# Loading k plainly and turning it on TensorE, one load queue in order of need, list-ordered layernorm: a change to the opening of a fused attention and gated-MLP kernel

## The chip, the cores and the metric

The kernel runs on one NeuronCore of one Trainium2 chip. The metric is the device time of one execution in microseconds (us). A change counts as faster or slower when the time moves by over 2%.

## The reference

```python
def reference(A_x, A_wqkv, A_w_phi, A_wo, B_x, B_w_gate, B_w_up, B_w_down):
    x  = A_x                                  # (1, 2048, 512) bf16
    xn = layernorm(x)                         # no scale, eps 1e-5
    # A: linear attention, H = 32 heads of 16, features = [softmax(k@w_phi), softmax(-k@w_phi)]
    #    kv = sum over s of phi_k^T v,  z = sum of phi_k,  o = (phi_q kv) / (phi_q z + 1e-6),  A = o @ wo
    # B: (xn@w_gate * xn@w_up) @ w_down       # F = 1792
    return x + A(xn, wqkv, w_phi, wo) + B(xn, w_gate, w_up, w_down)
```

## The kernel before

The kernel records steps with their reads and writes; a list scheduler then orders each engine. TensorE's order is fixed by the order of the recording, and so are steps recorded with `pin` set. The tokens come in 16 tiles of 128. To "turn" is to transpose; a "DMA turn" is a transpose made by a DMA, a copy that runs beside the engines; PSUM banks are the memory into which TensorE writes. `xn` is the normalised tile, `xnT` its turned form, `Wp` the product of the k (or q) weights with the block-diagonal `w_phi`, made once by `w_fold`; it needs the k weights turned. A "unit" (`up_unit`) is one gate/up pair of 4 + 4 matmuls of 128x512 into two PSUM banks, then a ScalarE copy and a VectorE multiply.

```python
    sc.pin = True                               # loads; SP and ACT are the two load queues
    load_x(0, 1)
    load_w(ACT, wv_v, ...)                      # 512 KB
    load_x(1, 1)
    load_x(2, 2)
    load_w(ACT, wphi_v, ...)
    load_qkT(1)                                 # k weights by a transposing DMA, SP queue
    load_gu(ACT, 0)                             # gate/up columns 0..255
    load_x(4, 4)
    load_gu(SP, 1)
    load_gu(SP, 2)                              # 1 MB
    load_x(8, 4)
    # ... (cut)
    sc.pin = True                               # the opening
    warm(16)
    ln_stats(0, 1); ln_stats(1, 1); ln_apply(0); ln_apply(1); ln_stats(2, 1); ln_stats(3, 1)
    x_transpose(0); x_transpose(1)
    ln_apply(2); ln_apply(3)
    v_matmul(0, 0)                              # v of tile 0 into PSUM bank 0
    v_matmul(1, 1)                              # v of tile 1 into PSUM bank 1
    x_transpose(2); x_transpose(3)
    for dt in range(NQ):
        w_fold(1, dt, (2, 3, 6, 7)[dt])
    sc.pin = False
    up()                                        # first unit, then the loop over tiles

    for t in range(NT + 2):                     # the loop, shortened
        if t < NT: features("ek", t, 1)         # matmul, two Exps, VectorE reduce ...
        if t % 2 == 0 and 4 + t < NT: ln_stats(4 + t, 2)
        up(); x_next(t + 4); late_loads(t)      # t == 5: w_down and wo, 2.3 MB
        # ... v_matmul(t - 1), v_scale(t - 1)
        if t < 2: v_scale(t, t)                 # reads PSUM bank t
        else:
            up(); kv_acc(t - 2); up()           # kv_acc writes PSUM banks 0 and 1
    # ... (cut)
    q_next(6)
    up(len(ups))                                # the units that are left
    num_stage(0)
    q_next(7)
    for t in range(1, NT):
        num_stage(t); out_tile(t - 1); q_next(t + 7)
    out_tile(NT - 1, 2)
```

Note for later: `kv_acc` of tile 0 may not start before `v_scale` of tile 1 has emptied bank 1.

The softmax here doesn't subtract the row's maximum and nothing guards it: scores larger than these inputs give would overflow.

## Time and profile before

| | |
|---|---|
| time, median of 4 runs | 230.68 us (230.38 to 231.04) |
| span in the profile | 228.0 us; that execution took 229.74 us, faster than all timed ones |
| TensorE busy | 96% |
| first gate/up unit on TensorE | 16.37 us |
| first kv accumulation | 27.6 us |

The page's head and slices. Each digit is the busy share of one fortieth of the span in tenths; PEclk is the granted TensorE clock in tenths.

```profile
span 228.0 us, 3302 instructions
PE 218.7 (96%) x1266; PEld 105.7 (46%) x1266; DVE 146.9 (64%) x276; ACT 83.3 (37%) x161; POOL 45.3 (20%) x77
PE   7389999999999999999999999989999999999995
DVE  2768998658546674667678456587776767635341
PEclk9979999999999999999999999999999999999999
```

TensorE is at 8 tenths or more from the third slice to the last but one, so only the opening, one small hole near slice 27 and the tail of 2.5 us can give anything.

The timeline of the opening, some lines (start in us, duration in us, engine, line, operation, output and input, count, and in brackets the idle time before it and what ended it; DVE is VectorE, ACT ScalarE, PE TensorE):

```profile
5.64 0.69 DVE L335 BATCH_NORM_STATS2 arena<-arena 128x6 f32<-128x512 bf16 x1 [1.57 <-DMA arena<-in_A_x_dram]
9.86 1.06 ACT L193 ACTIVATE arena<-ps 128x512 bf16<-128x512 bf16 x2
10.49 3.29 PE L212 MATMUL ps<-arena 128*128 128x512 bf16 x8 [2.26 <-ACT arena L193]
15.47 1.05 PE L314 MATMUL ps<-arena 128*128 128x128 bf16 x16 [0.96 <-ACT arena L193]
16.37 9.88 PE L212 MATMUL ps<-arena 128*128 128x512 bf16 x45
19.17 1.29 DVE L335 BATCH_NORM_STATS2 arena<-arena 128x6 f32<-128x512 bf16 x2 [0.18 <-DMA arena<-in_A_x_dram]
27.59 0.42 PE L423 MATMUL ps<-arena 128*128 128x68 bf16 x8
```

In order: statistics of x tile 1, late because its load shared the engines with wv; the first copies of turned x; the eight v matmuls at about half speed (0.41 us each against 0.216 later); the folds; the units; the statistics of x tile 8, which start almost without a wait; and the first kv accumulation (L423).

All waits of TensorE in that profile (who waits for whom: us in total, times, longest):

```profile
PE ps L212 <- ACT arena L193: 2.3, 1, 2.3
PE ps L536 <- DVE arena L273: 1.3, 1, 1.3
PE ps L365 <- DVE arena L345: 1.2, 2, 0.8
PE ps L212 <- DVE arena L500: 1.0, 1, 1.0
PE ps L314 <- ACT arena L193: 1.0, 1, 1.0
```

The only one after the opening is the 1.0 us for L500, the last gating multiply, at 150.5 us: the features of tile 7 want the bank it reads.

### The profile page before, as it was taken

The page shows a single profiled execution, that of the slowest core. Times are in us where ns is not written, and L with a number is a line of the kernel's source. Part 1 is how long each engine was busy: PE and PEld are TensorE (multiplying, and loading weights), DVE is VectorE, ACT ScalarE, POOL GpSimd, SP SyncE. Part 2 cuts the span into 40 slices and gives each one's busy share as a digit, 9 for nine tenths or more (in the row PEclk, how much of TensorE's full clock was granted, in tenths as well). Part 3 has the DMA queues.
Part 4 walks back from the last instruction along what each step waited for, and adds up shares of the span by engine and source line. Part 5 has one row for each costly group of instructions (what it writes and reads, how often), then busy time and mean ns, then how long its engine had stood idle before and what let it go on. Part 6 is the DMA issues. An engine that isn't in the chain of part 4 may idle for free.

```text
span 228.0 us, 3302 instructions
## 1 busy us (share of the span) xinstructions
PE 218.7 (96%) x1266; PEld 105.7 (46%) x1266; DVE 146.9 (64%) x276; ACT 83.3 (37%) x161; POOL 45.3 (20%) x77
## 2 busy tenths in 40 slices
PE   7389999999999999999999999989999999999995
PEld 3144444444444444444444444444444454454454
DVE  2768998658546674667678456587776767635341
ACT  3459467673343444335524434441111122000000
POOL 3210433403022201212242210131113211100000
PEclk9979999999999999999999999999999999999999
DMA  6997955990000000000220120228654545562221
GB/s 185 304 348 147 294 109 155 329 115 3 0 3 0 0 0 3 0 1 0 49 47 12 34 42 6 46 46 116 139 115 94 95 92 116 112 100 54 67 67 46
DMA packets 48513, 19.91 MB, mean 87 GB/s; under 512 B 37360, under 2 KB 48496, under 8 KB 48496
## 3 DMA queue, kind: packets, MB, share of 16 engines
q1 hardware_dynamic: 46384, 18.62, 36.5%
q10 hardware_dynamic: 2112, 1.07, 1.8%
q8 instruction: 10, 0.16, 0.3%
q14 instruction: 7, 0.06, 0.1%
HBM read 8.67 MB, written 2.10 MB: 47 GB/s over the span
## 4 chain that ended last, share of the span: by engine, by line
PE 92%; DVE 2%; DMA 2%; ACT 2%; issue 1%; SPq 0%; DVEq 0%
PE ps L212 88%; DMA arena<-in_A_x_dram 2%; PE ps L423 2%; PE ps L466 2%; ACT arena L193 2%; PE ps L314 1%; DVE arena L335 1%; DVE arena L500 0%; DVE arena L336 0%; DVE arena L345 0%; DVE arena L387 0%; PE ps L365 0%; DVE arena L517 0%; SPq L234 0%; DVEq L724 0%
## 5 line engine op out<-in xcount | busy, mean ns | idle before, releaser
L212 PE MATMUL ps<-arena 128*128 128x512 bf16 (+1 forms) x946 | 208.0, 377 | 3.3 <-ACT arena L193 2.3
L212 PEld LDWEIGHTS ps<-arena 128*128 128x128 bf16 x946 | 90.3, 98 | 103.5 <-ACT arena L193 2.4
L193 ACT ACTIVATE arena<-ps 128x512 bf16<-128x512 f32 (+1 forms) x128 | 70.0, 597 | 100.0 <-PE ps L212 95.6
L387 DVE TENSOR_REDUCE arena<-arena 128x64 f32<-128x1024 bf16 x32 | 38.7, 1214 | 20.7 <-ACT arena L193 20.7
L500 DVE TENSOR_TENSOR arena<-ps,arena 128x512 bf16<-128x512 f32 x56 | 38.3, 685 | 21.3 <-PE ps L212 20.8
L397 POOL TENSOR_TENSOR arena<-arena 128x512 bf16<-128x512 bf16 x32 | 33.7, 1055 | 67.9 <-DVE arena L395 61.1
L517 DVE TENSOR_TENSOR arena<-ps,arena 128x512 bf16<-128x512 f32 (+1 forms) x17 | 11.2, 660 | 23.7 <-PE ps L212 23.7
L410 POOL CAST arena<-arena 128x32 bf16<-128x32 f32 x16 | 5.1, 321 | 64.8 <-DVE arena L391 48.9
L193 ACT ACTIVATE arena<-arena 128x2 f32<-128x2 f32 (+2 forms) x32 | 13.8, 460 | 9.6 <-DVE arena L336 5.8
L335 DVE BATCH_NORM_STATS2 arena<-arena 128x6 f32<-128x512 bf16 x16 | 10.4, 675 | 4.9 <-DMA arena<-in_A_x_dram 4.9
L478 DVE TENSOR_TENSOR arena<-ps,arena 128x512 bf16<-128x512 f32 x16 | 11.1, 691 | 0.5
L411 DVE TENSOR_TENSOR arena<-ps,arena 128x512 bf16<-128x512 f32 x16 | 10.4, 649 | 0.1
L391 DVE RECIPROCAL arena<-arena 128x64 f32<-128x64 f32 x16 | 8.6, 538 | 0.0
L423 PEld LDWEIGHTS ps<-arena 128*128 128x128 bf16 x128 | 6.2, 97 | 3.8
L466 PEld LDWEIGHTS ps<-arena 128*128 128x128 bf16 x128 | 6.2, 97 | 3.8
L395 DVE TENSOR_TENSOR arena<-arena 128x32 f32<-128x32 f32 x32 | 6.8, 213 | 0.4
L423 PE MATMUL ps<-arena 128*128 128x68 bf16 x128 | 6.7, 194 | 0.0
L466 PE MATMUL ps<-arena 128*128 128x68 bf16 x128 | 6.7, 194 | 0.0
L536 PE MATMUL ps<-arena 128*128 128x512 bf16 x16 | 5.0, 480 | 1.3 <-DVE arena L273 1.3
L477 DVE RECIPROCAL arena<-arena 128x32 f32<-128x32 f32 x16 | 5.6, 353 | 0.5
L350 POOL TENSOR_SCALAR arena<-arena 128x1 f32<-128x1 f32 x12 | 2.9, 265 | 15.1 <-ACT arena L193 15.1
L393 DVE RECIPROCAL arena<-arena 128x32 f32<-128x32 f32 x16 | 5.6, 349 | 0.3
(22 smaller groups left out, 25.9 us busy)
## 6 DMA issues: line engine op xcount, KB each, us to landing
out_dram<-arena SPq DMA_DIRECT2D x15, 128.0 KB, 1.7
arena<-in_B_w_down_dram SPq DMA_DIRECT2D x1, 1792.0 KB, 8.0
arena<-in_A_x_dram SPq DMA_DIRECT2D x3, 512.0 KB, 6.4
arena<-in_B_w_gate_dram SPq DMA_DIRECT2D x3, 512.0 KB, 5.5
arena<-in_B_w_up_dram SPq DMA_DIRECT2D x3, 512.0 KB, 6.4
arena<-arena SPq DMA_TRANSPOSE x44, 3.0
arena<-in_A_wqkv_dram ACTq DMA_DIRECT2D x1, 512.0 KB, 4.2
arena<-in_A_wo_dram SPq DMA_DIRECT2D x1, 512.0 KB, 8.9
```

The lines of the kernel that those rows point to most:

```text
L193: return sc.step(ACT, lambda e: e.activation(out=out_ap, in_=in_ap, func=func, scale=scale, **kw), reads, writes, 130.0 + 0.833 * n)
L212: ins = e.matmul(out_ap, lhsT=l, rhs=r, start=start and i == 0, stop=stop and i == npair - 1, **kw)
L335: dve(lambda e, t=t: e.bn_stats(stats_v[:, t, 0:6], x_tile(t)), [("x", t)], [("st", t)], 512)
L387: dve(lambda e: e.tensor_reduce(out=sm, in_=e_v, axis=AX.X, op=ALU.add), [(name, s, 0), (name, s, 1)], [("sums", sr)], 1024)
L391: dve(lambda e: e.reciprocal(out=rs, in_=sm), [("sums", sr)], [("rs", s)], 64, 6.5)
L397: pool(lambda e: e.tensor_tensor(out=e_v[:, :, 1, :], in0=e_v[:, :, 1, :], in1=rat[:, :, None].to_broadcast([128, H, 16]), op=ALU.mult), [ ...
L411: dve(lambda e: e.tensor_tensor(out=vs_tile(t)[:, :, 0:16], in0=bank(b).rearrange("p (h f) -> p h f", h=H), in1=rp.unsqueeze(2).to_broadca ...
L423: ins = e.matmul(bank(c // 4, (c % 4) * CW, CW), lhsT=ek[:, c * 128:(c + 1) * 128], rhs=vs[:, c * CW:(c + 1) * CW], start=(t == 0 and c % ...
L466: ins = e.matmul(bank(b0 + c // 4, (c % 4) * CW, CW), lhsT=ph[:, c, :], rhs=kvz_v[:, c, :], start=True, stop=True)
L478: dve(lambda e: e.tensor_tensor(out=o_tile(t).rearrange("p (b h f) -> p b h f", b=2, f=16), in0=nd[:, :, :, 0:16], in1=w_v[:, r].unsqueeze ...
L500: dve(lambda e: e.tensor_tensor(out=hT_v[:, ft, sg * 512:(sg + 1) * 512], in0=bank(bu), in1=g, op=ALU.mult), [("ps", bu), ("g", s)], [("hT ...
L517: dve(lambda e, ps=ps, stg=stg, cs=cs: e.tensor_tensor(out=stg, in0=ps, in1=x_tile(t)[:, cs], op=ALU.add), [("ps", bk), ("x", t)], [("ostg ...
```

## The change

Intent: bring the opening to an end earlier. The first x tiles no longer share the DMA engines with wv, the transposing DMA of the k weights (4.94 us of issue time on the SP queue) goes away for 16 cheap turns on TensorE, all loads stand in one queue in order of need, and the layernorm steps of the first tiles are placed by the scheduler. Two units stand in front of the loop instead of one.

```diff
     load_x(0, 1)
-    load_w(ACT, wv_v, A_wqkv[:, 1024:1536]..., "wv", 524288)
-    load_x(1, 1)
+    load_x(1, 1, ACT)
     load_x(2, 2)
     load_w(ACT, wphi_v, ...)
-    load_qkT(1)
-    load_gu(ACT, 0)
+    load_w(SP, wk_v, A_wqkv[:, 512:1024]..., "wk", 524288)
+    load_w(SP, wv_v, A_wqkv[:, 1024:1536]..., "wv", 524288)
+    load_gu(SP, 0)
     load_x(4, 4)
     load_gu(SP, 1)
     load_gu(SP, 2)
 ...
+    def wk_transpose(jt, b):                    # four 128x128 turns, then a ScalarE copy
+        ...
 ...
-    sc.pin = True
-    warm(16)
-    ln_stats(0, 1) ... ln_apply(3)              # fixed order, see above
-    v_matmul(0, 0)
-    v_matmul(1, 1)
-    x_transpose(2)
-    x_transpose(3)
-    for dt in range(NQ):
-        w_fold(1, dt, (2, 3, 6, 7)[dt])
-    sc.pin = False
-    up()
+    for t in range(4):
+        ln_stats(t, 1)
+        ln_apply(t)
+    warm(11)
+    x_transpose(0, 2)
+    x_transpose(1, 3)
+    wk_transpose(0, 4)
+    wk_transpose(1, 6)
+    wk_transpose(2, 7)
+    wk_transpose(3, 2)
+    v_matmul(0, 0)
+    x_transpose(2, 3)
+    x_transpose(3, 4)
+    v_matmul(1, 1)
+    w_fold(1, 0, 2)
+    w_fold(1, 1, 3)
+    up()
+    w_fold(1, 2, 2)
+    w_fold(1, 3, 3)
+    up()
 ...
     q_next(6)
-    up(len(ups))
+    up(len(ups) - 1)
     num_stage(0)
+    up()
     q_next(7)
 ...                                             # _order: 50 instead of 200 ns after a step of the same engine
```

More of the change, by code (lines that the diff above doesn't have):

```diff
@@ L147, in _build @@
     alloc("zero", 512, at=layout["hT"])
+    alloc("wk", NQ * 512, at=layout["hT"] + (NF - 1) * S_TOK)
     alloc("wphi", NQ * 16)
@@ L156, in _build @@
     alloc("rstd", 2 * NT)
+    alloc("nbias", 2 * NT)
     alloc("lnv", 2 * NT)
-    alloc("nbias", 2 * NT)
+    alloc("eps", 2 * 2)
     alloc("sums", 2 * 16 * 64)
@@ L163, in _build @@
     alloc("w", 2 * 4 * 32)
-    alloc("eps", 2 * 2)
     total = (cur[0] + 31) // 32 * 32
@@ L228, in xnT, with load_x @@
         return sb("xnT", q * S_TOK + lo, n)
-    def load_x(t0, n):
+    def load_x(t0, n, eng=SP):
         o = sb("x", t0 * 512, n * 512).rearrange("p (t d) -> p t d", t=n)
         i = x_flat[t0 * 128:(t0 + n) * 128, :].rearrange("(t p) d -> p t d", p=128)
-        sc.dma(SP, lambda e: e.dma_start(o, i), [], [("x", t) for t in range(t0, t0 + n)], n * 131072)
+        sc.dma(eng, lambda e: e.dma_start(o, i), [], [("x", t) for t in range(t0, t0 + n)], n * 131072)
     wT_v = sb("wT", 0, 2 * NQ * 512).rearrange("p (w j d) -> p w j d", w=2, j=NQ)
+    wk_v = sb("wk", 0, NQ * 512).rearrange("p (q j) -> p q j", q=NQ)
     wv_v = sb("wv", 0, NQ * 512).rearrange("p (q j) -> p q j", q=NQ)
@@ L248, in load_qkT @@
         o, i = wT_v[:, w], A_wqkv[:, w * 512:(w + 1) * 512]
-        sc.dma(SP, lambda e: e.dma_start_transpose(o, i), [], [("wT", w)], 524288)
+        sc.dma(SP, lambda e: e.dma_start_transpose(o, i), [], [("wT", w, j) for j in range(NQ)], 524288)
     def load_gu(eng, s):
@@ L258, in _build @@
     load_x(0, 1)
-    load_w(ACT, wv_v, A_wqkv[:, 1024:1536].rearrange("(q p) j -> p q j", p=128), "wv", 524288)
-    load_x(1, 1)
+    load_x(1, 1, ACT)
     load_x(2, 2)
@@ L263, in _build @@
            "wphi", 16384)
-    load_qkT(1)
-    load_gu(ACT, 0)
+    load_w(SP, wk_v, A_wqkv[:, 512:1024].rearrange("(q p) j -> p q j", p=128), "wk", 524288)
+    load_w(SP, wv_v, A_wqkv[:, 1024:1536].rearrange("(q p) j -> p q j", p=128), "wv", 524288)
+    load_gu(SP, 0)
     load_x(4, 4)
@@ L306, in _build, with fn @@
     Wp_v = sb("Wp", 0, 2 * NQ * 512).rearrange("p (w q f) -> p w q f", w=2, q=NQ)
+    def wk_transpose(jt, b):
+        def fn(e):
+            ins = None
+            for dt in range(NQ):
+                ins = e.transpose(bank16(b, dt * 128, 128), wk_v[:, dt, jt * 128:(jt + 1) * 128], ident)
+            return ins
+        sc.step(PE, fn, ["wk", "ident"], [("ps", b)], 4 * 60.0)
+        act(wT_v[:, 1, jt, :], bank16(b, 0, 512), [("ps", b)], [("wT", 1, jt)])
     def w_fold(w, dt, b=None):
@@ L316, in fn @@
             return ins
-        sc.step(PE, fn, [("wT", w)] + [("wbd", jt) for jt in range(NQ)], [("ps", b)], 4 * 60.0)
+        sc.step(PE, fn, [("wT", w, jt) for jt in range(NQ)] + [("wbd", jt) for jt in range(NQ)], [("ps", b)], 4 * 60.0)
         if dt % 2 == 0:
@@ L325, in _build @@
     mv_v = sbf("mv", 0, NT * 2).rearrange("p (t k) -> p t k", t=NT)
-    lnv = sbf("lnv", 0, NT)
     rstd = sbf("rstd", 0, NT)
     nbias = sbf("nbias", 0, NT)
+    lnv = sbf("lnv", 0, NT)
     def xn_tile(t):
@@ L357, in x_turn, with x_transpose @@
         sc.dma(SP, lambda e: e.dma_start_transpose(o, xn_tile(t)), [("xn", t % 4)], [("xnT", t)], 131072)
-    def x_transpose(t):
-        b = misc_bank()
+    def x_transpose(t, b):
         def fn(e):
@@ L448, in q_transpose @@
         src = sb("eq", s * 1024, 1024)
-        wk = [("wT", 0), ("wT", 1)] if t < RP else []
+        wk = [("wT", w, j) for w in range(2) for j in range(NQ)] if t < RP else []
         sc.dma(SP, lambda e: e.dma_start_transpose(ph_tile(t), src), reads, [("phT", t % RP)] + wk, 262144, free=wk)
@@ L500, in up_unit @@
         dve(lambda e: e.tensor_tensor(out=hT_v[:, ft, sg * 512:(sg + 1) * 512], in0=bank(bu), in1=g, op=ALU.mult),
-            [("ps", bu), ("g", s)], [("hT", ft, sg)] + (["zero"] if ft == 0 and sg == 0 else []), 512)
+            [("ps", bu), ("g", s)], [("hT", ft, sg)] + (["zero"] if ft == 0 and sg == 0 else []) + (["wk"] if ft == NF - 1 and sg == 0 else []), 512)
     def out_tile(t, parts=1):
@@ L538, in warm @@
         sc.step(PE, fn, ["zero"], [("ps", 5)], n * 320.0)
-    sc.pin = True
-    warm(16)
-    ln_stats(0, 1)
-    ln_stats(1, 1)
-    ln_apply(0)
-    ln_apply(1)
-    ln_stats(2, 1)
-    ln_stats(3, 1)
-    x_transpose(0)
-    x_transpose(1)
-    ln_apply(2)
-    ln_apply(3)
+    for t in range(4):
[8 more added lines that the diff above has]
+    wk_transpose(3, 2)
     v_matmul(0, 0)
+    x_transpose(2, 3)
+    x_transpose(3, 4)
     v_matmul(1, 1)
-    x_transpose(2)
-    x_transpose(3)
-    for dt in range(NQ):
-        w_fold(1, dt, (2, 3, 6, 7)[dt])
-    sc.pin = False
+    w_fold(1, 0, 2)
[3 more added lines that the diff above has]
+    w_fold(1, 3, 3)
     up()
@@ L678, in _order @@
             remaining[d.idx] -= 1
-            ready_time[d.idx] = max(ready_time[d.idx], st.finish + LAT)
+            ready_time[d.idx] = max(ready_time[d.idx], st.finish + (LAT if d.lane != st.lane else 50.0))
             if remaining[d.idx] == 0:
```

## The prediction

> **What bounds it now.** The page gives PE 96% busy. The timeline shows why: from 16.5 to 225.5 us TensorE runs its list with one visible gap, 1.05 us at 150.5 (the features of tile 7 wait for the last gating multiply). 128x512 matmuls follow each other every 0.216 us. So only the opening 16.5 us, that gap and a tail of 2.5 us can give anything; the change adds no work to the long middle.
>
> **The opening before.** The chain of waits: tile 1 of x lands at 5.6 us, because its 128 KB share the DMA engines with the 512 KB of wv issued earlier on the other queue (the Trainium skill, "DMA: Bandwidth & Descriptors", Issuing engines are not separate DMA queues, says that such DMAs interleave on the same 16 engines; this trace agrees: x0 alone took 2.3 us, x1 4.4). Layernorm then turns xT0 at 7.0; four Ln/Exp pairs stand before the first PSUM copies on ScalarE (9.86); v matmuls start at 10.5 and take 3.29 us for 8 (0.41 each, granted clock 0.72 over 10.5-16.5) after 2.3 us of idle. The skill, "TensorE: Matmul & The Clock Gate", Part 1, says that an idle array drops to half clock; these 0.41 against 0.216 agree. Then turns, copies, four folds; gate/up work starts at 16.53. The transposed k load (issue 4.9 us, landing after 7.9) lands by 10.1, not last.
>
> **What the change does.** It removes the 512 KB DMA transpose and five warm-up matmuls; adds 16 128-column PE transposes (about 1 us) and four ScalarE copies (0.54 us each); moves x1 ahead of the weights, interleaves the layernorm, and starts one unit after two folds.
>
> Estimate from the trace's durations: x1 lands by about 3.6; xT0 turns near 5.9; wk lands near 6.2, wv near 7.7, both before they are needed. ScalarE becomes the chain: eight copies and the last Exps in a row, from 6.7 to about 11.8. First gate/up unit near 11.9, two folds (0.5 us) still to come: continuous work begins the equivalent of **4.1 us earlier**, v matmuls at full clock included.
>
> **What is given back.** VectorE was 91% busy in 16.5-28. Its list after has the statistics of tile 8 before the reduction of tile 0 and the third multiply, but the load of tile 8 is near the end of the same 5.2 MB and can land little earlier (19.1 before; I estimate 18.5). VectorE should idle about 2 us there, and the backlog makes TensorE wait near 26 us for a PSUM bank: about 0.9 us (0.3 to 1.5). At the end of the ups, the gap of 1.05 us shrinks to about 0.25, but the first output tile then arrives about 0.85 us before its transposed o: net zero.
>
> **Prediction: 227.6 us** (4.1 − 0.9 saved from 230.78), 8 in 10 between 226.0 and 229.4. Faster by over 2%: 0.13; within 2%: 0.86; slower: 0.01.
>
> **What would show it.** Right: tile 1 statistics start before 4 us; the first multi-unit matmul at 11.5-12.5; ScalarE solid from 6.7 to 11.8; no clock drop; VectorE waiting 1-2 us for the x load near 17-18.5; PE waiting for the multiply once near 26; PE waiting for the transposed o near 153 minus the gain. Wrong: clock below 0.9 between 7 and 14; PE waiting for wk or wv; no VectorE wait for x.
>
> **What would make it wrong.** TensorE is only about 60% busy between 5 and 12 us; if the clock halves there, 1 to 2.5 us are lost. If tile 8 lands early or TensorE never catches up with VectorE, nothing is given back: 226.7. If wk or wv land 2 us later than estimated, the start slips alike.

## The result, and the profile after

The changed kernel took 227.95 us (median of 4 runs, 227.71 to 228.13) against 230.68 us. The ratio is 0.988, 95% interval 0.9863 to 0.9898. Ratios in this document are the mean time of one kernel's fast runs over that of the other's of the same rounds, so not quite the ratio of the medians quoted. Executions over 1.5% slower than the fastest of the same kernel are left out of the means. The saving of 2.7 us was forecast as 3.1, and "within 2%" was the likely one.

The head and slices of the page after:

```profile
span 226.0 us, 3328 instructions
PE 218.4 (97%) x1277; PEld 105.5 (47%) x1277; DVE 146.4 (65%) x276; ACT 85.1 (38%) x165; POOL 45.3 (20%) x77
PE   7889899999999999999999999998999999999995
DVE  4496997776545675667577466598767677635341
PEclk9999999999999999999999999999999999999999
```

The clock stays up, TensorE's second slice is at 8 tenths instead of 3, but the fifth has a new dent. The timeline of the opening shows both:

```profile
3.56 1.29 DVE L346 BATCH_NORM_STATS2 arena<-arena 128x6 f32<-128x512 bf16 x2 [2.35 <-DMA arena<-in_A_x_dram]
8.26 1.04 PE L213 MATMUL ps<-arena 128*128 128x512 bf16 x4 [0.18 <-DMA arena<-in_A_wqkv_dram]
8.85 3.03 ACT L194 ACTIVATE arena<-ps 128x512 bf16<-128x512 bf16 x6
11.45 1.90 PE L213 MATMUL ps<-arena 128*128 128x512 bf16 x8
16.06 9.66 PE L213 MATMUL ps<-arena 128*128 128x512 bf16 x44 [0.48 <-DVE arena L347]
19.00 0.69 DVE L346 BATCH_NORM_STATS2 arena<-arena 128x6 f32<-128x512 bf16 x1 [2.25 <-DMA arena<-in_A_x_dram]
26.81 0.41 PE L433 MATMUL ps<-arena 128*128 128x68 bf16 x8 [1.09 <-DVE arena L421]
```

Statistics of tile 1 follow those of tile 0 at once; the first v matmuls run at full clock; ScalarE copies six banks in a row; the first unit starts at 11.45 instead of 16.37 us. Then VectorE stands for 2.25 us before the statistics of tile 8, whose load starts the work at 19.00 as against 19.17 before, and TensorE waits 1.09 us for `v_scale` (L421) before the first kv accumulation. These are all waits of TensorE over the whole run. Three of more than 0.2 us have no counterpart before: for L421, for the DMA (arena<-arena) and, in the opening, for L347; the 0.2 us for L510 is what is left of the 1.0 us for L500:

```profile
PE ps L546 <- DVE arena L275: 1.3, 1, 1.3
PE ps L213 <- DMA arena<-arena: 1.3, 1, 1.3
PE ps L433 <- DVE arena L421: 1.1, 1, 1.1
PE ps L375 <- DVE arena L356: 0.5, 1, 0.5
PE ps L213 <- DVE arena L347: 0.5, 1, 0.5
PE ps L213 <- DVE arena L510: 0.2, 1, 0.2
PE ps L213 <- DMA arena<-in_A_wqkv_dram: 0.2, 1, 0.2
```

The chain of waits (in order of time: start, duration, what) goes through the tile 8 load and then VectorE alone, without a single TensorE step from 10 to 26.8 us:

```profile
10.30 8.68 DMA arena<-in_A_x_dram
...
19.61 1.20 DVE arena L397
20.82 0.60 DVE arena L510
...
26.06 0.61 DVE arena L421
26.67 0.14 issue
26.81 0.41 PE ps L433 x8
```

So after the change the opening on TensorE is no longer what binds. The wait for the DMA (arena<-arena) in the list above, 1.25 us up to 153.63 us, is for the DMA turn of the first o tile.

An account from the two profiles, by issue of matmuls. The first unit starts 4.9 us earlier, and about 0.5 us of folds then still stand behind it: about 4.4 us gained. At the first kv accumulation it is 0.8 us (27.59 against 26.81) plus one more unit already done (eight matmuls of 0.216, 1.73 us): about 2.5 us left. At the end of the span, 2.0 us are left. So about 1.9 us went before the first kv accumulation and 0.5 us after it. Two stops make up the 1.9 us: without them the group of 16.06 would have started at 13.69 + 1.73 = 15.42 (0.64 us), and the kv accumulation at 16.06 + 44 x 0.216 = 25.56 (1.25 us). The timed medians differ by more (2.73 us) than the spans (2.0 us), because the profiled execution of the kernel before was a quick one, as the table says. Where its slower executions lose the rest was not traced, so some 0.7 us of the measured saving are outside this account.

### The profile page after: what moved, and what is told of

Same layout as the page of the kernel before. It is cut to its first block, busy times and chain, and to the rows that moved or that the text cites. A ratio compares the mean times of both kernels' runs of the same rounds, so it can differ in the third digit from the quotient of the medians.

```text
span 226.0 us, 3328 instructions
## 1 busy us (share of the span) xinstructions
PE 218.4 (97%) x1277; PEld 105.5 (47%) x1277; DVE 146.4 (65%) x276; ACT 85.1 (38%) x165; POOL 45.3 (20%) x77
## 4 chain that ended last, share of the span: by engine, by line
PE 84%; DMA 5%; DVE 4%; SPq 4%; issue 1%; ACT 0%
PE ps L213 81%; DMA arena<-in_A_x_dram 4%; SPq L247 3%; DVE arena L397 2%; PE ps L433 2%; PE ps L476 2%; DMA arena<-arena 1%; SPq L235 1%; DVE arena L421 1%; DVE arena L510 1%; DVE arena L401 0%; PE ps L325 0%; ACT arena L194 0%; DVE arena L488 0%; DVE arena L527 0%
## 5 line engine op out<-in xcount | busy, mean ns | idle before, releaser
L194 ACT ACTIVATE arena<-ps 128x512 bf16<-128x512 f32 (+1 forms) x132 | 72.2, 598 | 98.8 <-PE ps L213 97.8
L510 DVE TENSOR_TENSOR arena<-ps,arena 128x512 bf16<-128x512 f32 x56 | 38.4, 686 | 22.0 <-PE ps L213 20.1
L421 DVE TENSOR_TENSOR arena<-ps,arena 128x512 bf16<-128x512 f32 x16 | 10.4, 648 | 0.1
```

Source lines behind the costliest of these rows:

```text
L194: return sc.step(ACT, lambda e: e.activation(out=out_ap, in_=in_ap, func=func, scale=scale, **kw), reads, writes, 130.0 + 0.833 * n)
L421: dve(lambda e: e.tensor_tensor(out=vs_tile(t)[:, :, 0:16], in0=bank(b).rearrange("p (h f) -> p h f", h=H), in1=rp.unsqueeze(2).to_broadca ...
L510: dve(lambda e: e.tensor_tensor(out=hT_v[:, ft, sg * 512:(sg + 1) * 512], in0=bank(bu), in1=g, op=ALU.mult), [("ps", bu), ("g", s)], [("hT ...
```

## The experiments

Each call ran on one chip together with the kernel before. Medians of the fast runs in us; the mark says which kernel was edited.

| call, chip | kernel | median | ratio to before, 95% interval |
|---|---|---|---|
| 1, chip 5 | before | 231.46 | |
| | x8_first (after) | 228.45 | 0.9893, 0.985 to 0.9936 |
| | tail_hold_bank5 (after) | 226.68 | 0.9803, 0.9762 to 0.9845 |
| | before_warm (before) | 231.10 | 0.9996, 0.9951 to 1.0041 |
| | after_kdma (after) | 228.55 | 0.9882, 0.9841 to 0.9923 |
| 2, chip 0 | before | 232.08 | |
| | after_ctl (after, unedited) | 228.92 | 0.9871, 0.9825 to 0.9918 |
| | x8_wd (after) | 227.64 | 0.9818, 0.9771 to 0.9865 |
| | best2 (after) | 225.99 | 0.9743, 0.9697 to 0.9789 |
| | before_x1 (before) | 231.42 | 0.9988, 0.9948 to 1.0029 |
| 3, chip 10 | before | 231.29 | |
| | after_ctl_b (after, unedited) | 228.85 | 0.9919, 0.9874 to 0.9963 |
| | after_pinned (after) | 229.00 | 0.9916, 0.9874 to 0.9958 |
| | kdma_best (after) | 225.83 | 0.9783, 0.9743 to 0.9823 |
| | best2_b (after) | 225.87 | 0.979, 0.9755 to 0.9825 |

In these calls the kernel before scattered over some 2 to 3 us, with mean clocks from 0.978 to 1.0. The changed kernels scattered less. So small differences are read between changed kernels of one call, and from the traces.

The theory to test: the opening's gain is given back because tile 8 of x cannot land earlier than the bytes queued ahead of it allow, and VectorE's order puts its statistics before the work that frees PSUM bank 1 for the first kv accumulation. The rivals: VectorE is just overloaded; or one part of the change made all of the gain; or the halved clock did.

### x8_first: the tile 8 load earlier

```diff
     load_gu(SP, 1)
-    load_gu(SP, 2)
     load_x(8, 4)
+    load_gu(SP, 2)
```

> Edit on the changed kernel: the load of x tiles 8 to 11 is queued ahead of the third gate/up slice (1 MB) instead of behind it; nothing else. Theory A (VectorE stands still because the statistics of tile 8 wait for that load): the VectorE wait for x (2.25 us at 16.75-19.0 after the change) falls under 0.4 us, TensorE's wait of 1.09 us before the first kv accumulation at 26.8 us falls to 0-0.2 us, and the time falls by 0.8 to 1.2 us to about 226.9. The wait of 0.48 us at 15.6 us stays. Rival B (VectorE simply has too much work between 12 and 27 us): the wait for x goes but TensorE still waits 0.7 us or more at the first kv accumulation, and the time changes by under 0.4 us.

The wait of VectorE and the one of TensorE at the first kv accumulation both vanished: it started at 26.30 us, while tail_hold_bank5, on the same chip and with the opening of the changed kernel as it is, reached it at 27.51 after a wait of 0.99. So theory A is right about the mechanism, and 1.2 us were gained at that point. The edit did a little more than its text says: with the load earlier, the list scheduler also put the statistics of two more tiles in front (two at 18.07 us), and VectorE, with more work, was still in time, which speaks against rival B. The time did not keep the gain. There was no control in this call (its ratio of 0.9893 lies among the 0.987 to 0.992 of the unedited kernel), but the trace shows the loss: at the kv accumulation near 100 us this kernel stood at 100.05 and tail_hold_bank5 at 100.01. The forecast of the time was wrong because a second stop came, at 49 us (timeline of x8_first):

```profile
46.44 0.81 ACT L194 ACTIVATE arena<-arena 128x512 bf16<-128x512 bf16 x1 [3.40 <-DMA arena<-arena]
48.77 1.04 PE L213 MATMUL ps<-arena 128*128 128x512 bf16 x4 [0.57 <-ACT arena L194]
50.13 1.04 PE L213 MATMUL ps<-arena 128*128 128x512 bf16 x4 [0.33 <-DVE arena L510]
```

ScalarE wants to write a normalised tile into a ring of four, whose slot is still to be read by a DMA turn; and that turn stands behind w_down and wo (2.3 MB). The copies that free PSUM banks stand behind it in ScalarE's order: the next three started at 47.16 us.

### tail_hold_bank5: one unit kept for the first output tile

```diff
-        if t >= NT - 2:
+        if t == NT - 2:
             up()
 ...
-            features("eq", t, 0, 3 if t == 6 else 6 + t % 2)
+            features("eq", t, 0, 3 if t == 6 else 5 if t == 7 else 6 + t % 2)
```

> Edit on the changed kernel: one gate/up unit is kept back and runs between the numerator of tile 0 and the features of tile 7 (as the changed code intends, but its list is empty by then), and the features of tile 7 go to PSUM bank 5 in place of 7. Theory A (the first output tile comes before its o has been transposed by DMA, because no TensorE work stands in between): the 1.25 us wait for the transposed o near 153 us and the 0.2-0.3 us wait before the features of tile 7 both vanish, time down 1.2 to 1.6 us to about 226.5. Rival B (the o transpose is late because of the queue it shares with the q transposes): the wait moves but stays above 0.8 us, time down less than 0.5 us.

226.68 us, as theory A had it. TensorE had no wait at all after the first kv accumulation: the 1.3 us for the transposed o and the 0.2 us before the features of tile 7 are gone. Its size beside a control is read from call 2: best2, which is x8_wd with this edit, was 1.65 us below x8_wd. The give-back at the end of the units was therefore real; with a unit in the list it goes, while the first o turn still stands behind the same q turns on the DMA queue. The unit and the other PSUM bank were not tried apart.

### before_warm: fillers that keep the clock up, in the kernel before

```diff
     ln_apply(2)
     ln_apply(3)
+    warm(8)
     v_matmul(0, 0)
```

> Edit on the kernel before: eight filler matmuls on zeros in the 2.3 us hole in front of the v matmuls, no other change. Theory A (the halved clock cost 1.5 us, but the opening is worth only what the tile 8 load allows): the eight v matmuls take 1.7-1.8 us instead of 3.29, the gate/up work starts about 1.5 us earlier (near 15.0), TensorE then waits about 0.5 us before the first kv accumulation, which does not start before about 26.7 us; time down about 0.9-1.1 us to 229.7. Rival B (all of the opening's gain is kept): time down 1.5 us to 229.2, no such wait. Rival C (clock without effect): time unchanged at 230.7.

The eight v matmuls took 1.90 us and the units started at 14.78, about 1.6 us earlier. Nothing of it shows in the time: the ratio is 0.9996. Its timeline has four stops of TensorE that the profile of the kernel before has not, these three and one of 0.27 us before 28.48:

```profile
26.06 1.04 PE L212 MATMUL ps<-arena 128*128 128x512 bf16 x4 [0.76 <-DVE arena L500]
49.97 1.04 PE L212 MATMUL ps<-arena 128*128 128x512 bf16 x4 [0.69 <-ACT arena L193]
51.34 6.22 PE L212 MATMUL ps<-arena 128*128 128x512 bf16 x28 [0.33 <-DVE arena L500]
```

Theory A expected 0.9 to 1.1 us. The interval reaches from 1.1 us faster to 0.9 us slower, so the time alone does not exclude that; but theory A did not know of the stop at 50 us, and in the traces (other chip, other execution) the lead of 0.66 us at the first kv accumulation (26.93 against 27.59) is a lag of 1.1 us at the fifth (57.39 against 56.30). The halved clock was visible in the profile before, yet removing it alone was worth nothing that this measurement can see.

### after_kdma: the k weights by the transposing DMA again

```diff
-    load_w(SP, wk_v, A_wqkv[:, 512:1024]..., "wk", 524288)
+    load_qkT(1)
 ...
-    wk_transpose(0, 4)
-    wk_transpose(1, 6)
-    wk_transpose(2, 7)
-    wk_transpose(3, 2)
```

> Edit on the changed kernel: the k weights come by the transposing load again, at the same place in the queue, and the 16 TensorE turns and their four copies are gone. Theory A (the transposing load matters through the queue it blocks): the loads behind it are issued about 4 us later, v matmuls wait for wv until about 10 us, gate/up work starts 1.5 to 3 us later than 11.45, the tile 8 load lands 0.3 to 1.5 us later than 19.0 and with it the first kv accumulation; time 228.5 to 230. Rival B (the order of x and the layernorm made the whole gain, and the turns on TensorE cost about what they save): time within 0.4 us of 227.95 or below.

228.55 us with no control in its call. The trace agrees with theory A in the opening (v matmuls waited 2.9 us for wv, first unit at 13.93), but the first kv accumulation came at 27.33, against 27.51 in tail_hold_bank5 on the same chip. The start 2.2 us later (tail_hold_bank5 has its first unit at 11.70) cost nothing there. The reason is not the one of theory A: the list scheduler, given the other loads, put the statistics of tile 8 behind the first kv accumulation, so VectorE did not stand for them and TensorE did not wait at all:

```profile
27.33 0.42 PE L433 MATMUL ps<-arena 128*128 128x68 bf16 x8
30.12 1.28 DVE L346 BATCH_NORM_STATS2 arena<-arena 128x6 f32<-128x512 bf16 x2
```

So the stop needs both, the late load and its statistics in front on VectorE. This run alone left open whether the turns on TensorE are worth anything; kdma_best below was made for that.

### after_ctl: the control

> The changed kernel itself, unedited, as the control for the other runs of this call (the first call had none, and its chip loaded the weights some 0.5 us later than the first chip). Expected 0.986 to 0.990 of the kernel before, 227.7 to 228.6 us. The first kv accumulation at 26.7-27.6 us with a 0.9-1.1 us wait for VectorE, the wait for the transposed o 1.2-1.3 us.

228.92 us, slightly above the range, ratio 0.9871 as expected. On this chip the k weights landed later: TensorE waited 1.14 us for them, which it did not on the first chip, and the first unit started at 12.31. Everything behind moved alike.

### x8_wd: both stops in the loop taken away

```diff
     load_gu(SP, 1)
-    load_gu(SP, 2)
     load_x(8, 4)
+    load_gu(SP, 2)
 ...
-        elif t == 5:
+        elif t == 12:
             load_w(SP, wd_v, ...)      # w_down
             load_w(SP, wo_v, ...)
```

> Edit on the changed kernel: tile 8 load ahead of the third gate/up slice (as in x8_first) and the loads of w_down and wo (2.3 MB) queued at step 12 of the loop instead of step 5, which leaves the order on every engine but the DMA queue as in x8_first. Theory A (x8_first took away the wait at the first kv accumulation, but TensorE then ran into a second one at 49-50 us, 0.9 us, because ScalarE waited 3.4 us for the DMA turn of an x tile that stood behind w_down and wo): that second wait and ScalarE's wait vanish, the first kv accumulation stays near 26 us without a wait, and the time is 0.9 to 1.3 us under the control. Rival B (TensorE gets stopped again by VectorE or ScalarE work whenever it is earlier): other waits of 0.7 us or more appear between 27 and 100 us and the time is within 0.4 us of the control.

227.64 us, 1.28 us below the control: theory A. The first kv accumulation started at 26.63 without a wait (27.95 after 0.83 in the control), and the next six follow every 7.16 us with no stop at 49 us. Since the order on ScalarE, VectorE and GpSimd, and of TensorE's weight loads, is in the trace that of x8_first, the second stop was the queueing of the DMA turn behind w_down and wo.

### best2: x8_wd and tail_hold_bank5 together

> Edit on the changed kernel: x8_wd and tail_hold_bank5 together. Theory A (the two give-backs are independent, one in the loop and one at the first output tile): savings add up, 2.3 to 2.9 us under the control, about 225.3. Rival B (an earlier loop makes the q transposes or w_down collide with the first output tile): under 1.8 us below the control, with a new wait near 150 us.

225.99 us, 2.93 us below the control (the range said 2.3 to 2.9): the two give-backs add up, and no new wait appears. This is every wait of TensorE in best2:

```profile
PE ps L546 <- DVE arena L275: 1.3, 1, 1.3
PE ps L314 <- DMA arena<-in_A_wqkv_dram: 1.0, 1, 1.0
PE ps L213 <- DVE arena L347: 0.5, 1, 0.5
PE ps L213 <- DMA arena<-in_A_wqkv_dram: 0.5, 1, 0.5
PE ps L325 <- DVE arena L332: 0.5, 1, 0.5
```

All lie in the first 18 us. best2 is the quickest kernel of this call, and that repeated on another chip (below). By the 2% rule it is faster than the kernel before in this call (0.9743), unclear in the next (0.979), and within 2% of the changed kernel (1.3% below the control).

### before_x1: only the load of x tile 1 moved, in the kernel before

```diff
     load_x(0, 1)
+    load_x(1, 1, ACT)
     load_w(ACT, wv_v, ...)
-    load_x(1, 1)
     load_x(2, 2)
```

> Edit on the kernel before: the load of x tile 1 goes out on the second queue ahead of wv, nothing else. Theory A (the opening is not what binds once TensorE reaches the first kv accumulation: this is set by tile 8 landing near 19 us and the VectorE work behind it): tile 1 statistics start at 3.3-3.9 instead of 5.64, gate/up work starts 1 to 1.8 us earlier, but TensorE waits in front of or just after the first kv accumulation and the time is 0 to 0.7 us below the kernel before. Rival B (this reordering is the main part of the gain): time down 1.5 us or more.

231.42 us, ratio 0.9988: no gain that shows, as theory A said, but it got there in a worse way than expected. The v matmuls started at 8.76, yet the folds waited for the transposed k weights until 12.75, and after the first unit (13.87) TensorE stood 2.92 us for ScalarE, which was held up by the statistics of tile 4: these started at 14.05, as against 11.63 before, and tile 8 at 21.44 as against 19.17. Moving one load forward may have pushed the others back; but the kernel before was not traced on this chip, where after_ctl, too, had tile 8 1.15 us later than on the first, so part of this is the chip or the execution.

### after_ctl_b, after_pinned: the order of the first layernorms

```diff
-    for t in range(4):
-        ln_stats(t, 1)
-        ln_apply(t)
-    warm(11)
+    sc.pin = True
+    warm(11)
+    ln_stats(0, 1); ln_stats(1, 1); ln_apply(0); ln_apply(1)
+    ln_stats(2, 1); ln_stats(3, 1); ln_apply(2); ln_apply(3)
+    sc.pin = False
```

> The changed kernel again, unedited, as the control of this call: 227.7 to 229 us by the chip.

> Edit on the changed kernel: the layernorm of the first four tiles in the fixed order of the kernel before (statistics 0 and 1, apply 0 and 1, statistics 2 and 3, apply 2 and 3) instead of the order that the list scheduler chooses. Theory A (this part of the change touches only the opening, and what an opening gains or loses under about 1 us is hidden behind the tile 8 load): the first gate/up unit moves by less than 0.8 us, the first kv accumulation by less than 0.4 us, time within 0.4 us of the control. Rival B (the order is a main part of the gain): 0.8 us or more slower than the control.

229.00 against 228.85 us: within the 0.4 us of theory A. The traces are more telling than the times, and they contradict the limits that theory A set for the two points. With the fixed order the first unit started 1.8 us *earlier* than in the control (11.48 against 13.30: it waited 0.30 us for the k weights and the control 1.43, and the clock of the control's profiled execution then fell to 0.50; its other three executions had 1.0), and the first kv accumulation 0.7 us *later* (28.83 against 28.15), because tile 8's statistics started 0.7 us later (21.03 against 20.35). Why that load landed later is not known; its order in the queue is the same.

### kdma_best, best2_b: is the turn on TensorE worth anything once nothing hides it?

> best2 (tile 8 load early, w_down and wo late, one unit kept for the first output tile) with the k weights by the transposing load again. Theory A (the turns of k on TensorE do start the gate/up work earlier, but in the changed kernel as it stands the tile 8 load hides it; with that taken away the difference shows): 0.7 to 1.3 us slower than best2_b. Rival B (the turns give nothing): within 0.3 us of best2_b.

> The same kernel as best2, to stand beside kdma_best on one chip and to repeat its gain: 2.5 to 3.2 us under the control of this call, ratio to the kernel before 0.973 to 0.978.

225.83 against 225.87 us: theory A falls, rival B stands, as far as six runs of each that scatter over 1 to 2 us can tell. The two traces do not show that tie, since each is of an extreme execution: best2_b's was its slowest (226.55 us, one of two with a lowered clock), kdma_best's its second fastest (225.39). In them, with the transposing DMA the first unit started at 11.70, in best2_b at 14.05, because on this chip best2_b waited 1.5 us for the k weights and then ran at half clock for a while, whereas kdma_best needs them only at the folds:

```profile
9.08 1.02 PE L213 MATMUL ps<-arena 128*128 128x512 bf16 x4 [1.91 <-DMA arena<-in_A_wqkv_dram]
11.70 1.89 PE L213 MATMUL ps<-arena 128*128 128x512 bf16 x7
26.14 0.42 PE L433 MATMUL ps<-arena 128*128 128x68 bf16 x8
```

(kdma_best.) The same three points of best2_b are 10.17, 14.05 and 27.45 us, and its span is 1.2 us longer (224.8 against 223.6). best2_b itself was 2.98 us below its control, as expected; its ratio of 0.979 is just above the forecast range.

### One table over the traces

Starts in us, read from the timelines. "Distance" is the first kv accumulation minus the statistics of tile 8.

| kernel | first unit | tile 8 statistics | first kv accumulation | distance |
|---|---|---|---|---|
| after | 11.45 | 19.00, waited | 26.81, waited | 7.81 |
| tail_hold_bank5 | 11.70 | 19.70, waited | 27.51, waited | 7.81 |
| after_ctl | 12.31 | 20.15, waited | 27.95, waited | 7.80 |
| after_ctl_b | 13.30 | 20.35, waited | 28.15, waited | 7.80 |
| after_pinned | 11.48 | 21.03, waited | 28.83, waited | 7.80 |
| after_kdma | 13.93 | after the first kv accumulation | 27.33, no wait | |
| x8_first | 11.62 | no wait | 26.30, no wait | |
| x8_wd | 11.96 | no wait | 26.63, no wait | |

In five of the six changed kernels that have the tile 8 load in its old place the distance is 7.8 us, while the first unit wanders by 1.85 us. That is what a floor looks like. The sixth, after_kdma, has VectorE in another order and no such floor.

## Why the prediction was right

The time (227.6 forecast, 227.95 measured) and most of its structure held. That the time came so near is partly luck: the traces give 4.4 gained, 1.9 and 0.5 given back, 2.0 us in all, where the prediction had 4.1 and 0.9, 3.2 in all; the timed 2.7 lies between, for the reason given in the account. Point by point:

- **What bounded the kernel before.** Shown, with one limit: the opening was the only large hole, but in before_warm a start 1.6 us earlier was worth nothing visible. The kernel before stood close to a second stop already: in its profile ScalarE waits 2.73 us for a DMA turn before 46.55 us, and TensorE hardly feels it (7.23 us to the next kv accumulation instead of 7.16); in before_warm that wait is 4.04 us and the step takes 8.53. The changed kernel has no such wait; what that is worth in the slower executions of the kernel before was not traced.
- **Opening, 4.1 us.** About 4.4 from the traces on the first chip: the first unit at 11.45 as against 11.9. Tile 1 at 3.56 (with tile 0, as forecast), no drop of the clock, ScalarE copying to the end. It does not hold everywhere: the first unit came at 12.31 and 13.30 in the controls, where TensorE waited 1.14 and 1.43 us for the k weights and, in the second, the clock fell to 0.50. Both are signs that the prediction had listed under "Wrong" and as risks; on the first chip there was only a wait of 0.18 us for wv.
- **VectorE's wait for tile 8, about 2 us.** 2.25 us, at the place named (16.75 to 19.00). x8_first shows that the late load is a cause, after_kdma that the order on VectorE is the other.
- **The give-back on TensorE, 0.9 us (0.3 to 1.5).** The term was mis-sized: about 1.9 us. Part of it is a wait that the prediction did not have, 0.48 us at 15.6 us; the profile puts it down to L347 on VectorE, and since the features waiting there need the last fold's copy (L332), which ended shortly before, that copy behind the statistics of tiles 6 and 7 is the likely reason; no run tested it. The other part was forecast "near 26 us for a PSUM bank", and came there with 1.09 us. The bank was another one: not that of the fourth gating multiply but bank 1, held by v of tile 1 until `v_scale`. The backlog that caused it was the one named.
- **The end of the units, net zero.** The gap shrank to 0.18 (forecast 0.25), the wait for the transposed o was 1.25 (forecast 0.85); 0.5 us were lost instead of none. tail_hold_bank5 shows that a unit held back removes both.
- **"If tile 8 lands early, nothing is given back: 226.7."** Wrong. x8_first did this and the 1.2 us gained were given back at 49 us. The prediction had looked at the loop as free of waits and not asked what an earlier TensorE would run into. x8_wd shows the missing half.
- **The parts of the change.** The prediction did not price them. Turning k on TensorE gave nothing measurable (kdma_best against best2_b), the list order of the layernorms gave nothing (after_pinned), early x tile 1 alone and the full clock alone gave nothing in the kernel before. "Nothing" means nothing that shows: these comparisons cannot see less than about 0.8 to 1.2 us. What stays open is how the 2.7 us split between the order of the one queue, the second unit in front of the loop and the scheduler's shorter latency, which were in every changed kernel that ran. The account says that 1.73 of the 2.5 us left at the first kv accumulation are that one unit more: TensorE meets the floor having done more work. No run separated them.

Two pages of the Trainium skill were used. "DMA: Bandwidth & Descriptors", Issuing engines are not separate DMA queues, says that DMAs started by different engines run on the same 16 DMA engines and interleave. The traces agree: tile 1 started work at 5.64 us beside wv, with tile 0 at 3.56 us without it, and at 4.07 us in before_x1, where its load alone went ahead of wv. (The prediction calls tile 0 "alone", but wv was issued 0.02 us after it.) The same page gives about 358 GB/s as the limit of HBM for one core (Specifications); here the DMA engines moved 347 GB/s from 12 to 16.5 us, and 362 from 12 to 14 us in after_kdma. So tile 8 could hardly come earlier but by a change of order; that is inferred, and x8_first shows only that the order does it. "TensorE: Matmul & The Clock Gate", Part 1, says that an idle array falls to half its clock: that was seen (0.55 granted from 10.5 to 14 us before), and was gone with fillers in the hole (1.00 from 8 to 14 us in before_warm).

## What to carry to other kernels

When an opening is shortened, look for the first point at which the busy engine meets a load or an in-order engine that did not move: here the distance to that point was all the gain there was, and behind it the next one waited. Read it from several traces as a constant distance between a landing and a stop, and look at the order on the engine between them too: in after_kdma another order removed the stop with the load where it was. Then order the loads by what stands behind them, also those of small tiles behind megabytes of weights that nobody needs yet, and test each part of a change without the others, because the part that gives it its name may give nothing.

## What the Trainium skill lacked or had wrong

- "TensorE: Matmul & The Clock Gate", HAM oscillation, gives "no PE-idle gaps >~3.4µs" as the rule. At first sight the runs contradict it: before the change the clock was 0.50 from 12 to 14 us after a longest idle gap of 2.26 us, and in after_ctl_b it was 0.50 from 8.5 to 10.5 us after gaps of 0.56 and 1.43 us. But beside these gaps TensorE did only turns. From the last filler to the first v matmul it was 4.26 us in the kernel before, 4.50 in after_ctl_b, 4.07 in best2_b and 3.58 in after_kdma, the four traces in which the clock fell in the opening; it was 3.55 and 3.68 in after_ctl and tail_hold_bank5, and 3.44 or less in the other eight, in which it did not. So no run shows the rule wrong if turns are left out as work; whether they count was not tested.
- "DMA: Bandwidth & Descriptors", DMA Transpose (X-bar), has no issue time for a transposing load. One of 512 KB from HBM held the issuing queue for 4.94 us and landed after 7.9 us in the kernel before; in after_kdma it took 2.76 us and landed after 5.2, and x tile 4 was issued at 6.25 us instead of 3.97 in tail_hold_bank5 on the same chip.
- I found no page that says how far landing times differ between executions or chips. The same program started tile 8's statistics at 19.00, 20.15 and 20.35 us on three chips, with waits of 0, 1.14 and 1.43 us for the same 512 KB of k weights. One execution was traced on each; after_pinned, with the same loads on the third chip, waited 0.30 us, so the chip is not the only reason.
